# 256 rows of w2 by an indirect load to 64 chosen partitions, in a fused adaLN, cached attention and MLP decode step

## The chip, the cores and the metric

One core of a Trainium2 chip runs the whole program. The metric is device time in microseconds (us) of one execution, the median of several runs. The profiled execution is one more run, with its own time.

## What is computed

Eight tokens (one for each sequence, D = 512) go through attention over a window of a key and value cache and then through an MLP, each with an adaptive layer norm and a gate from a conditioning vector c.

```python
mod = (silu(c) @ w_mod).reshape(8, 6, 1, -1)            # sa, ca, ga, sb, cb, gb
h = layernorm(x) * (1 + ca) + sa
q = (h @ wq)                                             # 32 heads of 128
k, v = k_cache[:, :, Sk - W:], v_cache[:, :, Sk - W:]    # W = 2048 of 8192, 8 kv heads
o = softmax(q k^T * Dh ** -0.5) v
x = x + ga * (o @ wo)
h = layernorm(x) * (1 + cb) + sb
r = relu(h @ w1 + b1) ** 2                               # w1 [512, 1792]
x = x + gb * (r @ w2 + b2)                               # w2 [1792, 512]
```

All of it is float32. The caches' windows are 134 MB, the weights some 31 MB, and each byte is used once.

## The kernel before

Four slots of 4 MB in SBUF (`slots`) hold whatever is being used: two halves of w_mod, two of wq, then for each of the eight sequences two tiles of K and two of V, then wo (two tiles), w1 and w2. `load` issues the transfers of one such tile on SyncE's queue (SP), and `pump` issues the next tile of the list as soon as a slot comes free, so the order of all bulk transfers is the list `loads`. SP also waits for the completion of the transfer that used the same one of eight completion semaphores before.

The loop over b (line 431 on) overlaps three stages: turning K by 32x32 transposes on VectorE (`turn`), `scores` on TensorE with a block query matrix in `qb`, the softmax (`rows`, `maximum`, `exponent`, `divisor`, `spread`), and P times V of the sequence before (`turn_p`, `weighted`, `gather`).

The tail, from line 473 on, is: the product with wo; the residual and the second norm; h2T, the second norm's result with its columns turned onto partitions; `ph`, the hidden layer; relu, square, a 32x32 transpose (rT); and the product with w2.

The 1792 rows of w2 are held in two ways. The main part has FC rows on each of 128 partitions (FC = 13, 1664 rows, line 109), loaded in five pieces (line 110): f = 0 to 3, 4 to 7, 8 to 10, 11, 12. The other 128 rows are the extra part: four rows on each of 32 partitions, in `w2x`, the storage of the query matrices, which are dead after the last scores. A memset of Pool's (line 325) clears it first, and two transfers on SP (line 108, EXTRA) fill it. The hidden layer is split the same way: `ph` has the 13 x 32 columns of each quarter on 128 partitions, and `px` (line 529) has the extra 128 columns, with relus on ScalarE (line 545) and a transpose into rxT (line 555).

The product with w2 has three parts. (1) f = 0 to 3 and the four extra rows are eight products of 512 columns in four column groups of the array, which end in `wy_ps` (line 562); these are copied to `at_y` by VectorE (left half) and then by ScalarE (right half; lines 566 and 567) and summed over the four groups by products with `sel` (line 579). (2) f = 4 to 7 are products of 128 columns, one for each quarter of D, straight into `py` (line 572). (3) f = 8 to 12 are such quarters too, issued after the sums. `y` is py times the gate plus x1 (lines 585 and 586), and goes out by one transfer.

A product in float32 stands in the trace as two matrix instructions, so eight instructions are four products.

## Time and profile before

| | us |
|---|---|
| median of 3 runs (391.48 to 391.55) | 391.51 |
| the profiled execution | 391.81 |
| its span, first to last instruction | 390.0 |

| engine | busy us | share of the span |
|---|---|---|
| TensorE | 257.2 | 66% |
| VectorE | 215.7 | 55% |
| ScalarE | 42.8 | 11% |
| GpSimd (Pool) | 6.6 | 2% |
| SP's transfer queue, of 16 DMA engines | | 98.4% |

165.05 MB are moved, 423 GB/s over the span. A busy share is an average over stages; which wait ends last in a stage is read from the chain of waits and from the timeline. The granted clock is TensorE's; a share of 1.00 is 2.4 GHz, 0.50 is 1.2 GHz.

### The profile page before, as it was taken

Reading aid. Unit: us, or ns where it says so; the run is one execution under the profiler, and the core shown is the slowest. Engines: PE = TensorE matmul, PEld = TensorE weight load, DVE = VectorE, ACT = ScalarE, POOL = GpSimd, SP = SyncE. Lnnn points to the kernel's source line nnn. Section 1 sums busy time; section 2 is a strip of 40 time slices with the busy share of each in tenths; the row PEclk is TensorE's granted clock in tenths of the full one; section 3 lists DMA queues with packets and bytes.
Section 4 is the critical chain, followed back from the end, with each engine's and each line's share of the span. In section 5 each row is a group of like instructions: output and inputs, shape, how many; then the busy total and the mean of one; then the engine's idle time right before and its main releaser. Section 6 shows DMA issues by size and latency. Waiting matters only on the chain.

```text
span 390.0 us, 4820 instructions
## 1 busy us (share of the span) xinstructions
PE 257.2 (66%) x2126; PEld 111.1 (28%) x2126; DVE 215.7 (55%) x234; ACT 42.8 (11%) x91; POOL 6.6 (2%) x14
## 2 busy tenths in 40 slices
PE   0272808678975694859485938394749475985975
PEld 0120201151351343124322422233223313452332
DVE  3420199399394939293928391939292938330032
ACT  0310100030030003000300020003000300032010
POOL 4000000000000000000000000000000000100000
PEclk9998758969975986889778987797688779888889
DMA  8999999999999999999999999999999999999995
GB/s 325 432 434 428 430 430 434 434 444 439 435 437 428 427 432 434 430 428 430 429 430 428 434 430 432 437 439 430 439 434 434 426 437 425 434 435 413 424 421 207
DMA packets 7253, 165.05 MB, mean 423 GB/s; under 512 B 888, under 2 KB 1056, under 8 KB 1696
## 3 DMA queue, kind: packets, MB, share of 16 engines
q1 hardware_dynamic: 7096, 164.70, 98.4%
q8 instruction: 17, 0.28, 0.3%
q10 hardware_dynamic: 72, 0.04, 0.0%
q14 instruction: 4, 0.03, 0.0%
q0 software_dynamic: 64, 0.00, 0.0%
HBM read 164.67 MB, written 0.07 MB: 422 GB/s over the span
## 4 chain that ended last, share of the span: by engine, by line
DMA 53%; DVE 25%; PE 20%; ACT 1%; issue 1%; DVEq 0%; ACTq 0%; SPq 0%
DMA slot<-in_A_k_cache_dram 34%; DVE slot L307 22%; PE s_ps L317 16%; DMA slot<-in_B_w_dram 9%; DMA slot<-in_A_wq_dram 7%; DMA slot<-in_w_mod_dram 3%; PE t_ps L260 2%; PE t_ps L388 1%; PE o_ps L400 1%; PE m_ps L276 1%; DVE pT L389 0%; ACT prd L378 0%; DVE s L331 0%; DVE s L335 0%; DVE mx L340 0%
## 5 line engine op out<-in xcount | busy, mean ns | idle before, releaser
L307 DVE STREAM_TRANSPOSE slot<-slot 128x2048 f32<-128x2048 f32 x64 | 143.9, 2284 | 41.7 <-DMA slot<-in_A_k_cache_dram 41.7
L317 PE MATMUL s_ps<-slot,qb_all 128*32 128x512 f32 x512 | 121.7, 1099 | 68.4 <-DVE slot L307 67.5
L317 PEld LDWEIGHTS s_ps<-slot,qb_all 128*32 128x32 f32 x512 | 22.3, 136 | 147.7 <-issue 82.1
L400 PE MATMUL o_ps<-slot,pT 128*32 128x256 f32 x1024 | 59.7, 382 | 0.0
L400 PEld LDWEIGHTS o_ps<-slot,pT 128*32 128x32 f32 x1024 | 46.0, 112 | 27.7 <-issue 18.8
L388 PE MATMUL t_ps<-ident,prd 128*128 128x128 f32 x128 | 27.1, 373 | 16.5 <-ACT prd L378 9.5
L331 DVE STREAM_TRANSPOSE s<-s_ps 128x512 f32<-128x512 f32 x8 | 5.7, 717 | 54.2 <-PE s_ps L317 54.2
L388 PEld LDWEIGHTS t_ps<-ident,prd 128*128 128x128 f32 x128 | 20.2, 189 | 22.3 <-ACT prd L378 21.8
L378 ACT ACTIVATE prd<-pr,rz 128x512 f32<-128x512 f32 x32 | 20.5, 710 | 9.4 <-DVE rz L370 9.4
L354 ACT ACTIVATE pr<-s,nm 128x512 f32<-128x512 f32 x8 | 5.8, 722 | 141.2 <-DVE nm L348 141.2
L389 DVE TENSOR_TENSOR pT<-t_ps,m 128x512 f32<-128x512 f32 x32 | 20.4, 670 | 1.3 <-PE t_ps L388 1.2
L410 ACT COPY o_sb<-o_ps 128x256 f32<-128x256 f32 x16 | 5.8, 363 | 122.1 <-PE o_ps L400 122.1
L260 PE MATMUL t_ps<-slot,h1T 128*32 128x512 f32 x64 | 9.8, 764 | 8.9 <-DMA slot<-in_A_wq_dram 6.9
L475 PE MATMUL s_ps<-slot,oT 128*32 128x512 f32 x56 | 8.5, 773 | 4.5 <-DMA slot<-in_A_wo_dram 4.5
L173 PE MATMUL m_ps<-xsum,sel 128*128 128x1 f32 x2 | 0.6, 362 | 16.5 <-DVE xsum L196 16.5
L294 DVE TENSOR_TENSOR qb_all<-qrep,block 128x512 f32<-128x512 f32 x8 | 9.0, 1124 | 3.0 <-ACT qrep L286 3.0
L272 DVE STREAM_TRANSPOSE qT<-t_ps 128x512 f32<-128x512 f32 x2 | 1.4, 717 | 15.9 <-PE t_ps L260 15.7
L366 PE MATMUL m_ps<-z,same 128*128 128x1 f32 x16 | 3.3, 273 | 9.5 <-ACT pr L354 9.5
L238 PE MATMUL m_ps<-slot,cT 128*32 128x384 f32 x64 | 7.8, 658 | 0.0
L325 POOL MEMSET qb_all<- 64x2048 f32 x1 | 1.8, 1807 | 331.9 <-PE s_ps L317 331.9
L489 DVE COPY at_i<-s_ps 128x256 f32<-128x256 f32 x1 | 0.4, 425 | 12.2 <-PE s_ps L475 12.2
L260 PEld LDWEIGHTS t_ps<-slot,h1T 128*32 128x32 f32 x64 | 2.4, 133 | 16.1 <-DMA slot<-in_A_wq_dram 7.8
(113 smaller groups left out, 102.5 us busy)
## 6 DMA issues: line engine op xcount, KB each, us to landing
slot<-in_A_k_cache_dram SPq DMA_DIRECT2D x16, 4096.0 KB, 18.6
slot<-in_A_v_cache_dram SPq DMA_DIRECT2D x16, 4096.0 KB, 28.2
slot<-in_A_wq_dram SPq DMA_DIRECT2D x2, 4096.0 KB, 26.4
slot<-in_w_mod_dram SPq DMA_DIRECT2D x2, 3072.0 KB, 17.2
slot<-in_A_wo_dram SPq DMA_DIRECT2D x1, 4096.0 KB
slot<-in_A_wo_dram SPq DMA_DIRECT2D x1, 2048.0 KB
slot<-in_A_wo_dram SPq DMA_DIRECT2D x2, 1024.0 KB
slot<-in_B_w_dram SPq DMA_DIRECT2D x2, 1024.0 KB
```

Of the source, the lines that this page charges most:

```text
L238: nc.tensor.matmul(pm[i][32 * q : 32 * q + 32, : 3 * P].rearrange("p (m n) -> p m n", m=3), cT[:, kc, :], wm[:, 3 * i : 3 * i + 3, q, :], ...
L260: nc.tensor.matmul(pq[t][32 * x : 32 * x + 32, :], hT[:, kc, :], w[:, 2048 * t + 512 * x : 2048 * t + 512 * x + 512], start=(kc == 0), sto ...
L294: nc.vector.tensor_mul(qb[b % 2][:, :, :, :REP], qrep_b[:, :, None, :, b].to_broadcast([P, 32, 4, REP]), block[:, None, :, None].to_broadc ...
L307: nc.vector.transpose(k, k)
L317: nc.tensor.matmul(S_[b][32 * x : 32 * x + 32, :].rearrange("p (j i) -> p j i", i=8), q[:, n : n + 32], k[:, :, c, :, x], start=(t == 0 an ...
L354: nc.scalar.activation(pr.rearrange("p j (a i) -> p j a i", a=4), S2_.pop(b).rearrange("p (a j i) -> p j a i", a=4, i=8), AF.Exp, bias=NM_ ...
L378: nc.scalar.activation(d, pr[:, 4 * n : 4 * n + 4, :, None].to_broadcast([P, 4, 32, 4]), AF.Copy, scale=RZ_[b][0])
L388: nc.tensor.transpose(pp[:, P * i : P * i + P], d[:, i].rearrange("p i u -> p (i u)"), one)
L389: nc.vector.tensor_mul(PT_[b][:, n].rearrange("p q j (x r) -> p q (j x) r", r=REP), pp.rearrange("p (y q r) -> p q y r", y=16, r=REP), m16 ...
L400: nc.tensor.matmul(o[32 * (m % 4) : 32 * (m % 4) + 32].rearrange("p u d -> p (u d)"), PT_[b][:, n, 2 * q + t, 2 * u : 2 * u + 2, :].rearra ...
L410: nc.scalar.copy(O_[b][:, t], o)
L475: nc.tensor.matmul(wo_ps[32 * (i % 4) : 32 * (i % 4) + 32, :], oT[:, i, :], slot(("wo", i // 16), D)[:, i % 16, :], start=(i < 4), stop=(i ...
```

## The change

FC goes from 13 to 12, so the main part of w2 is 1536 rows in pieces f = 0 to 3, 4 to 7, 8 and 9, 10, 11, and the extra part is 256 rows: four on each of 64 partitions. These 64 are not a block: `EXTRA` names runs of partitions in the four groups of 32. The rows come by one indirect transfer of Pool's, behind a memset of all 128 partitions, right after the last scores; its list of row numbers (`places`) is made at the start by a memset and nine iotas of Pool's and two operations of VectorE's, and holds an out-of-range number for the 64 partitions that get nothing. SP's two transfers of extra rows go. The bias loads move from the program's start to ScalarE's queue in the second batch (b = 1).

In the tail, the product of b1_x comes before the hidden layer's loop; `px` has 256 columns on all 128 partitions; six relus take the place of two; the square and the transpose of rx come after both halves of r; f = 4 to 7 become products of 512 columns in `wy_ps`, eight in place of four of the main part; at_y is two tiles; f = 8 and 9 come before the sums, f = 10 and 11 after.

TensorE in the tail, before (s_ps is wy_ps, t_ps is ph and then py, m_ps is px; slot_90 holds w2):

```order
L520 MATMUL t_ps<-slot_91,h2T 32x416 x16
L527 MATMUL m_ps<-b_x,ident 64x128
L529 MATMUL m_ps<-slot_91,h2d 64x128 x4
L562 MATMUL s_ps<-slot_90,rT 32x512 x4
L562 MATMUL s_ps<-qb_all,rxT 32x512 x4
L569 MATMUL t_ps<-b_in,fours 128x128
L572 MATMUL t_ps<-slot_90,rT 32x128 x16
L579 MATMUL t_ps<-at_y,sel 32x128 x4
L572 MATMUL t_ps<-slot_90,rT 32x128 x20
```

and now (slot_87 holds w2):

```order
L550 MATMUL m_ps<-b_x,ident 128x256
L553 MATMUL t_ps<-slot_88,h2T 32x384 x16
L561 MATMUL m_ps<-slot_88,h2d 128x256 x4
L593 MATMUL s_ps<-slot_87,rT 32x512 x8
L593 MATMUL s_ps<-qb_all,rxT 32x512 x4
L600 MATMUL t_ps<-b_in,fours 128x128
L604 MATMUL t_ps<-slot_87,rT 32x128 x8
L611 MATMUL t_ps<-at_y_1825,sel 32x128 x2
L611 MATMUL t_ps<-at_y_1826,sel 32x128 x2
L604 MATMUL t_ps<-slot_87,rT 32x128 x8
```

Sixteen quarters of f = 4 to 7 have become four products of 512 columns, which stand ahead of the extra rows' four and of the sums. What these wait for now (DMAHW3 is the landing of w2's second piece, DMASW0 that of the indirect transfer):

```order
L593 MATMUL s_ps<-slot_87,rT 32x512 [waits DMAHW3_49]
L593 MATMUL s_ps<-slot_87,rT 32x512
L593 MATMUL s_ps<-slot_87,rT 32x512 [waits DVE_49]
L593 MATMUL s_ps<-slot_87,rT 32x512
L593 MATMUL s_ps<-qb_all,rxT 32x512 [waits DMASW0_49,DVE_49]
L593 MATMUL s_ps<-qb_all,rxT 32x512 x3
```

The extra rows' products, which before waited only for rxT and their own rows, are now behind the second piece of w2 too.

ScalarE at the end of the tail, before and now (rx is the extra part of r):

```order
L542 ACTIVATE relu<-t_ps 128x32x6
L542 ACTIVATE relu<-t_ps 128x32x7
L545 ACTIVATE rx<-m_ps 32x4x5x4
L545 ACTIVATE rx<-m_ps 32x4x3x4
L567 COPY at_y<-s_ps 128x256
```

```order
L574 ACTIVATE relu<-t_ps 128x32x6 [waits PE_49]
L574 ACTIVATE relu<-t_ps 128x32x6
L577 ACTIVATE rx<-m_ps 32x128 [waits PE_49,Pool_49]
L577 ACTIVATE rx<-m_ps 32x128
L577 ACTIVATE rx<-m_ps 32x24
L577 ACTIVATE rx<-m_ps 32x16 x3
L598 COPY at_y_1826<-s_ps 128x256 [waits DVE_49,Activation_49]
```

The relus are four more, and the copy of the right half of wy_ps waits, as before, for VectorE's copy of the left half, though the two now write two tiles.

SP's last transfers, before and now:

```order
L108 DMA qb_all<-in_B_w_dram 20x1x2048
L108 DMA qb_all<-in_B_w_dram 12x1x2048
L114 DMA slot_90<-in_B_w_dram 128x2048 x2
L114 DMA slot_90<-in_B_w_dram 128x1536
L114 DMA slot_90<-in_B_w_dram 128x512 x2
```

```order
L119 DMA slot_87<-in_B_w_dram 128x2048 x2
L119 DMA slot_87<-in_B_w_dram 128x1024
L119 DMA slot_87<-in_B_w_dram 128x512 x2
```

The extra rows are gone from SP's queue, and the third piece is a third shorter. The diff, cut to its core:

```diff
--- before.py
+++ after.py
@@ -41,7 +41,7 @@
     F = w1.shape[1]
     NJ = W // 32
     NQ = D // P
-    FC = F // P - 1
+    FC = F // P - 2
     FG = FC * 32
     FX = F - P * FC
     SCALE = float(DH) ** -0.5
@@ -61,15 +61,24 @@
     nc.vector.memset(xc_in, 0.0)
     for q in range(NQ):
         nc.scalar.dma_start(xc_in[32 * q : 32 * q + B], xc[32 * q : 32 * q + B])
-    b1_in = consts.tile([NQ, FG], F32, name="b1_in")
+    b1_in = consts.tile([NQ, FG + 32], F32, name="b1_in")[:, :FG]
     b1_x = consts.tile([1, FX], F32, name="b1_x")
     b2_in = consts.tile([NQ, P], F32, name="b2_in")
-    nc.scalar.dma_start(b1_in, b1[: P * FC].rearrange("(g n) -> g n", g=NQ))
-    nc.gpsimd.dma_start(b1_x, b1[P * FC :].rearrange("(g n) -> g n", g=1))
-    nc.gpsimd.dma_start(b2_in, b2.rearrange("(g n) -> g n", g=NQ))
-
-
-    EXTRA = ((0, 5, P * FC, 0), (32, 3, P * FC + 80, 80))
+
+
+    EXTRA = (
+        (0, 0, 12, 0),
+        (0, 16, 4, 16),
+        (0, 28, 4, 28),
+        (1, 0, 20, 32),
+        (1, 26, 6, 58),
+        (2, 0, 6, 52),
+        (2, 28, 4, 12),
+        (3, 0, 4, 20),
+        (3, 28, 4, 24),
+    )
+
+    SPAN = ((0, 0, 32, 0), (1, 0, 32, 32)) + EXTRA[5:]
     qb_all = consts.tile([P, 2, 32, 4, 8], F32, name="qb_all")
     w2x = qb_all.rearrange("p t n a z -> p (t n a z)")
 
@@ -102,12 +111,8 @@
             v = w1.rearrange(r_kc, p=P)
             pieces = [(lo, v[:, lo:hi]) for lo, hi in ((0, 2), (2, 3), (3, 4))]
         else:
-
-            for g, o, first, _ in EXTRA:
-                v = w2[first : first + 16 * o].rearrange("(i o c) n -> o i (c n)", i=4, o=o)
-                nc.sync.dma_start(w2x[g : g + 4 * o, :], v)
             v = w2[: P * FC].rearrange("(p c) n -> p c n", p=P)
-            cuts = ((0, 4), (4, 8), (8, 11), (11, 12), (12, 13))
+            cuts = ((0, 4), (4, 8), (8, 10), (10, 11), (11, 12))
             pieces = [(lo, v[:, lo:hi]) for lo, hi in cuts]
         for lo, v in pieces:
             a, n = v.shape[1:]
...
@@ -221,7 +226,22 @@
     qb = [qb_all[:, i] for i in range(2)]
     for t in qb:
         nc.gpsimd.memset(t, 0.0)
-    rx = consts.tile([64, 32, 4], F32, name="rx")
+
+    place_r = work.tile([P, 32], F32, name="mt", bufs=1)
+    nc.gpsimd.memset(place_r, float(F))
+    for g, l, n, first in EXTRA:
+        nc.gpsimd.iota(
+            place_r[32 * g : 32 * g + 1, l : l + n],
+            pattern=[[1, n]],
+            base=P * FC // 4 + first,
+            channel_multiplier=0,
+            allow_small_or_imprecise_dtypes=True,
+        )
+    place_c = work.tile([P, 32], F32, name="nm")
+    nc.vector.transpose(place_c, place_r)
+    places = consts.tile([P, 1], mybir.dt.uint32, name="places")
+    nc.vector.tensor_copy(places, place_c[:, 0:1])
+    rx = consts.tile([P, 32, 4], F32, name="rx")
     nc.gpsimd.memset(rx, 0.0)
     oT = consts.tile([P, 32, 32], F32, name="oT")
     nc.gpsimd.memset(oT, 0.0)
@@ -322,7 +342,15 @@
                     stop=(t == 1 and c == 3),
                 )
         if b == B - 1 and t == 1:
-            nc.gpsimd.memset(w2x[:64, :], 0.0)
+            nc.gpsimd.memset(w2x, 0.0)
+            nc.gpsimd.indirect_dma_start(
+                w2x,
+                None,
+                w2.rearrange("(r c) n -> r (c n)", c=4),
+                bass.IndirectOffsetOnAxis(ap=places[:, :1], axis=0),
+                bounds_check=F // 4 - 1,
+                oob_is_err=False,
+            )
         done(("K", b, t))
 
     def rows(b):
@@ -465,6 +493,10 @@
             exponent(b)
         else:
             nc.scalar.activation(warm, eps, AF.Sqrt)
+        if b == 1:
+            nc.scalar.dma_start(b1_in, b1[: P * FC].rearrange("(g n) -> g n", g=NQ))
+            nc.scalar.dma_start(b1_x, b1[P * FC :].rearrange("(g n) -> g n", g=1))
+            nc.scalar.dma_start(b2_in, b2.rearrange("(g n) -> g n", g=NQ))
         if b > 0:
             weighted(b - 1, 1)
     gather(B - 1)
@@ -507,14 +539,15 @@
     xm, rstd = norm(x1, x1sum)
     nc.vector.tensor_mul(xm, xm, mods[1][:, 1, :])
     h2T = scaled(xm, rstd, mods[1][:, 0, :], "h2T")
-    h2d = work.tile([P, NQ, 2, 32], F32, name="h2d", tag="prd", bufs=4)
-    nc.vector.tensor_copy(h2d, h2T[:, :, None, :].to_broadcast([P, NQ, 2, 32]))
+    h2d = work.tile([P, NQ, 4, 32], F32, name="h2d", tag="prd", bufs=4)
+    nc.vector.tensor_copy(h2d, h2T[:, :, None, :].to_broadcast([P, NQ, 4, 32]))
 
     w1t = slot(("w1",), F)
     w2t = slot(("w2",), D)
     ph = ps_t.tile([P, 512], F32, name="t_ps")
     px = bank()
     nc.tensor.matmul(ph[:, :FG], four, b1_in, start=True, stop=False)
+    nc.tensor.matmul(px[:, :FX], one[:1, :1].to_broadcast([1, P]), b1_x, start=True, stop=False)
     for kc in range(NQ):
         for g in range(NQ):
             nc.tensor.matmul(
@@ -524,10 +557,9 @@
                 start=False,
                 stop=(kc == NQ - 1),
             )
-    nc.tensor.matmul(px[:64, :FX], one[:1, :1].to_broadcast([1, 64]), b1_x, start=True, stop=False)
     for kc in range(NQ):
         nc.tensor.matmul(
-            px[:64, :FX],
+            px[:, :FX],
             h2d[:, kc].rearrange("p a b -> p (a b)"),
             w1t[:, kc, P * FC :],
             start=False,
@@ -535,51 +567,51 @@
         )
     r = work.tile([P, 32, FC], F32, name="relu", tag="a")
     rT = work.tile([P, FC, 32], F32, name="rT", bufs=1)
-    rxT = work.tile([64, 4, 32], F32, name="rxT", bufs=1)
+    rxT = work.tile([P, 4, 32], F32, name="rxT", bufs=1)
     h = ph[:, :FG].rearrange("p (l c) -> p l c", l=32)
     halves = ((0, 6), (6, FC))
     for lo, hi in halves:
         nc.scalar.activation(r[:, :, lo:hi], h[:, :, lo:hi], AF.Relu)
 
-    for g, o, _, at_ in EXTRA:
+    for g, l, k, first in SPAN:
         nc.scalar.activation(
-            rx[g : g + 32, : 4 * o, :].rearrange("p (o i) c -> p i o c", i=4),
-            px[g : g + 32, at_ : at_ + 16 * o].rearrange("p (i o c) -> p i o c", i=4, o=o),
+            rx[32 * g : 32 * g + 32, l : l + k, :],
+            px[32 * g : 32 * g + 32, 4 * first : 4 * (first + k)].rearrange("p (l c) -> p l c", c=4),
             AF.Relu,
         )
     for lo, hi in halves:
         nc.vector.tensor_mul(r[:, :, lo:hi], r[:, :, lo:hi], r[:, :, lo:hi])
         nc.vector.transpose(rT[:, lo:hi], r[:, :, lo:hi].rearrange("p l c -> p c l"))
-        if lo == 0:
-            nc.vector.tensor_mul(rx, rx, rx)
-            nc.vector.transpose(rxT, rx.rearrange("p l c -> p c l"))
+    nc.vector.tensor_mul(rx, rx, rx)
+    nc.vector.transpose(rxT, rx.rearrange("p l c -> p c l"))
 
 
     wy_ps = ps_s.tile([P, D], F32, name="s_ps")
-    chunks = [(rT[:, f, :], w2t[:, f, :]) for f in range(4)]
-    chunks += [(rxT[:, c, :], w2x[:64, D * c : D * c + D]) for c in range(4)]
+    chunks = [(rT[:, f, :], w2t[:, f, :]) for f in range(8)]
+    chunks += [(rxT[:, c, :], w2x[:, D * c : D * c + D]) for c in range(4)]
     for i, (left, right) in enumerate(chunks):
         nc.tensor.matmul(
-            wy_ps[32 * (i % 4) : 32 * (i % 4) + 32, :], left, right, start=(i < 4), stop=(i >= 4)
-        )
-    at_y = work.tile([P, D], F32, name="at_y", tag="a")
-    nc.vector.tensor_copy(at_y[:, : D // 2], wy_ps[:, : D // 2])
-    nc.scalar.copy(at_y[:, D // 2 :], wy_ps[:, D // 2 :])
+            wy_ps[32 * (i % 4) : 32 * (i % 4) + 32, :], left, right, start=(i < 4), stop=(i >= 8)
+        )
+    at_y = [work.tile([P, 2, P], F32, name=f"at_y{i}", tag="prd", bufs=4) for i in range(2)]
+    nc.vector.tensor_copy(at_y[0], wy_ps[:, : D // 2].rearrange("p (q n) -> p q n", q=2))
+    nc.scalar.copy(at_y[1], wy_ps[:, D // 2 :].rearrange("p (q n) -> p q n", q=2))
     py = ps_t.tile([P, 512], F32, name="t_ps")
     nc.tensor.matmul(py[:, :P], four, b2_in, start=True, stop=False)
+
     def quarters(f, last):
         for q in range(NQ):
             nc.tensor.matmul(
                 py[32 * q : 32 * q + 32, :P], rT[:, f, :], w2t[:, f, q * P : (q + 1) * P], start=False, stop=last
             )
 
-    for f in range(4, 8):
+    for f in range(8, 10):
         quarters(f, False)
     for q in range(NQ):
         nc.tensor.matmul(
-            py[32 * q : 32 * q + 32, :P], sel[:, :32], at_y[:, q * P : (q + 1) * P], start=False, stop=False
-        )
-    for f in range(8, FC):
+            py[32 * q : 32 * q + 32, :P], sel[:, :32], at_y[q // 2][:, q % 2, :], start=False, stop=False
+        )
+    for f in range(10, FC):
         quarters(f, f == FC - 1)
     y = work.tile([P, P], F32, name="y", bufs=1)
     nc.vector.tensor_mul(y, py[:, :P], mods[1][:, 2, :])
```

## Rows read from the trace of the kernel before

**Rows 1.** The chain of waits, its last pieces: start us, us, what.

```profile
376.05 10.34 DMA slot<-in_B_w_dram
...
386.43 0.47 PE t_ps L572 x8
...
386.93 0.30 DVE y L585
```

**Rows 2.** Stretches of the tail: us, busy time by engine, clock, DMA share, GB/s.

```profile
370.70:374.40 3.70, 1.64 (x8) 0.90 (x9) 2.28 (x10) 0.76 (x3) 0.00 (x0) 1.00 0.99 418
...
374.90:378.10 3.20, 3.20 (x24) 0.65 (x12) 0.00 (x0) 0.00 (x0) 0.00 (x0) 0.50 1.02 429
...
381.00:383.40 2.40, 2.40 (x22) 0.60 (x24) 1.84 (x5) 0.01 (x1) 0.00 (x0) 1.00 0.94 392
383.40:387.00 3.60, 2.77 (x81) 1.92 (x80) 0.19 (x2) 0.38 (x1) 0.00 (x0) 1.00 0.49 189
```

**Rows 3.** DMA issues: sizes in KB, and us from issue to landing.

```profile
slot<-in_A_k_cache_dram SPq DMA_DIRECT2D x16, 4096.0 KB, 18.6
...
slot<-in_B_w_dram SPq DMA_DIRECT2D x1, 768.0 KB
slot<-in_B_w_dram SPq DMA_DIRECT2D x2, 256.0 KB, 10.3
```

**Rows 4.** Timeline of PE in the tail: start us, us, instructions [idle before <-releaser].

```profile
378.57 0.53 PE L520 MATMUL t_ps<-slot,h2T 128*32 128x416 f32 x4
...
379.39 1.09 PE L529 MATMUL m_ps<-slot,h2d 128*64 128x128 f32 x8
380.96 1.07 PE L562 MATMUL s_ps<-slot,rT 128*32 128x512 f32 x8 [0.49 <-DMA slot<-in_B_w_dram]
381.96 1.06 PE L562 MATMUL s_ps<-qb_all,rxT 64*32 64x512 f32 x8
...
383.37 1.08 PE L572 MATMUL t_ps<-slot,rT 128*32 128x128 f32 x32
```

**Rows 5.** Timeline of ScalarE (ACT) and VectorE (DVE) in the tail.

```profile
380.57 0.44 ACT L545 ACTIVATE rx<-m_ps 32x80 f32<-32x80 f32 x2 [0.80 <-PE m_ps L529]
...
381.05 0.28 DVE L554 TENSOR_TENSOR rx<-rx 64x128 f32<-64x128 f32 x1 [0.58 <-ACT rx L545]
381.36 0.41 DVE L555 STREAM_TRANSPOSE rxT<-rx 64x128 f32<-64x128 f32 x1
...
383.09 0.42 DVE L566 COPY at_y<-s_ps 128x256 f32<-128x256 f32 x1 [0.45 <-PE s_ps L562]
...
383.61 0.38 ACT L567 COPY at_y<-s_ps 128x256 f32<-128x256 f32 x1 [2.59 <-DVE at_y L566]
```

**Rows 6.** Timeline near 45 us: eight matrix instructions with 128x128 weights and 256 columns.

```profile
45.67 1.99 PE L276 MATMUL m_ps<-qT,rep 128*128 128x256 f32 x8 [0.85 <-DVE qT L272]
```

**Rows 7.** Timeline of the product with wo and its sums, at full clock.

```profile
365.25 0.14 PEld L475 LDWEIGHTS s_ps<-slot,oT 128*32 128x32 f32 x4 [0.29 <-issue]
365.68 0.13 PEld L475 LDWEIGHTS s_ps<-slot,oT 128*32 128x32 f32 x4 [0.29 <-issue]
...
368.97 0.37 ACT L490 COPY at_i<-s_ps 128x256 f32<-128x256 f32 x1 [14.24 <-DVE at_i L489]
...
369.39 0.14 PEld L493 LDWEIGHTS m_ps<-at_i,sel 128*32 128x32 f32 x4 [0.26 <-ACT at_i L490]
...
369.58 1.10 PE L498 MATMUL m_ps<-slot,oT 128*32 128x128 f32 x32
370.73 0.29 DVE L505 TENSOR_TENSOR x<-m_ps,mod 128x128 f32<-128x128 f32 x1 [1.79 <-PE m_ps L498]
```

**Rows 8.** Timelines: start of the program, second batch, and just after the last scores.

```profile
3.07 0.32 ACTq L67 DMA_DIRECT2D b_in<-in_B_b_dram  x1
...
111.50 1.95 ACT L378 ACTIVATE prd<-pr,rz 128x512 f32<-128x512 f32 x3 [1.23 <-DVE rz L370]
...
337.85 1.81 POOL L325 MEMSET qb_all<- 64x2048 f32 x1 [331.91 <-PE s_ps L317]
```

More of the change, by code (lines that the diff above doesn't have):

```diff
@@ L199, in tile_adaln_cached_attention_mlp @@
     nc.scalar.activation(warm, eps, AF.Exp)
-    rep = consts.tile([P, 4, 4, 32], F32, name="rep")
+    rep = work.tile([P, 4, 4, 32], F32, name="rep", tag="prd", bufs=4)
     nc.vector.tensor_copy(
```

## The prediction

> **What bounds the kernel now.** I read the chain of waits first. Its last pieces are a transfer of w2 that lands at 386.39 (376.05 + 10.34), eight matrix instructions of the last quarter at 386.43, and y at 386.93 [rows 1]. So the end is the last landing plus 0.54 us up to y, and what follows y is not touched. The stretches of the tail say how that transfer ends: from 374.9 to 378.1 the 16 DMA engines are all busy (share 1.02 at 429 GB/s), from 381.0 to 383.4 the share is 0.94, and from 383.4 to 387.0 only 0.49 [rows 2]. The engines run dry one after another: 0.49 of 3.6 us is 1.76 us of work for all sixteen, so with the same bytes shared evenly the last would land near 383.4 + 1.76 = 385.16 and not at 386.39. That is the most that a better sharing can give, 1.2 us. The timeline then shows what TensorE, ScalarE and VectorE have to do between the landings [rows 4, 5].
>
> **The change, part by part.**
>
> *The transfers.* Bytes are the same. The main part of w2 loses one row in thirteen, 256 KB, all in the third piece (768 KB before [rows 3], 512 now); these and the 256 KB of the old extra part become the indirect load's 512 KB. For an engine that gets none of the 64 rows that is 16 KB less behind the second piece; an engine moves 429 / 16 = 26.8 GB/s [rows 2], so it ends 0.61 us sooner, and a row of 8 KB costs an engine 0.31 us. If the engines that end last now get none or few of the rows, the last landing goes from 386.39 to 385.78. I take this; the bounds are 385.16 (even sharing) and 388.2 (eight rows, 2.45 us, on an engine that is among the last now, less 0.61).
>
> The second piece ends where it did, since it and all before it in SP's queue are unchanged on those engines. It has landed by 383.37, when its first quarter product runs [rows 4], and not much sooner: 768 + 256 + 256 KB lie behind it [rows 3], which is 1.31 MB or 3.05 us at 430 GB/s before 386.39, so 383.34.
>
> *Pool.* The memset is as wide per partition as before (1.81 us from 337.85 [rows 8]), so the indirect load is issued near 340, and its rows are wanted after 384: whatever Pool needs to work out 64 rows is hidden by 40 us. The iotas, and VectorE's two small operations, stand in the first 20 us, where bulk loads run anyway.
>
> *The biases.* Three issues on ScalarE at about 0.32 us each [rows 8] come to 1.0 us in the second batch. ScalarE sat idle for 1.23 us there [rows 8], but its copy of the output tile is now behind them, and TensorE's gather behind that, so up to 1 us of one batch may move. A K tile lands 18.6 us after its issue [rows 3], while moving its own 4.19 MB takes 9.8 us at 429 GB/s: some 9 us are queued ahead, and that cover hides it. Were it gone, the cost would be that 1 us.
>
> *The extra part of the hidden layer.* w1's last piece is no later, so px's products start near 379.0, the end of the last products of L520 (378.57 + 0.53 = 379.10 [rows 4], less 0.06 for 384 in place of 416 columns). Eight instructions with 128x128 weights and 256 columns took 1.99 us [rows 6], where px takes 1.09 [rows 4]: it ends at 381.0. The relu follows 0.09 us after the end (380.48 to 380.57 [rows 4, 5]); two took 0.44, six take 1.32, up to 382.4. Square, transpose and their two gaps take 0.72 (381.05 to 381.77 [rows 5], and 0.04 before): rxT is ready at 383.2, against 381.77 before. That is 1.4 us later, but the extra rows' products are now behind f = 4 to 7, which can't start before 383.37 and stream for 0.86 us. So I cost this at nothing; the slack is 384.2 - 383.2 = 1.0 us.
>
> *The products of 512 columns.* This is what now ends late. f = 4 to 7 start at 383.37, and the extra rows' four follow. In the trace eight instructions at 381.96 let VectorE's copy go at 383.09, 1.13 us [rows 4, 5]; eight more, streamed, add 2 x 0.43 us (the pace of four, 365.25 to 365.68 [rows 7]): 383.37 + 1.13 + 0.86 = 385.36. The copy of the left half and the wait behind it take 0.52 (383.09 to 383.61) and ScalarE's copy of the right half 0.38 [rows 5]: 386.26. Two tiles don't make these run side by side, since the order shows the second still waiting for VectorE.
>
> *The sums and the last quarters.* The same step after wo: the copy ends at 369.34, the sum's second half starts at 369.39, and VectorE's next operation at 370.73, 1.34 us, with 32 instructions of quarters in 1.10 us behind the sum [rows 7]. Now 16 follow (f = 10 and 11), 0.55 less: 0.79. So y starts at 386.26 + 0.05 + 0.79 = 387.10, against 386.93: **0.2 us later**. By the transfer alone it would be 385.78 + 0.54 = 386.32, so the landing that ended the kernel is now hidden by 0.8 us and the chain from w2's second piece ends it.
>
> **The sum.** 391.51 + 0.2 = 391.7. The sum is made on the profiled execution, whose 391.81 would become 392.0; the median is 0.30 below it. Terms I am unsure of by some tenths are the landing of the second piece and the pace of the copies. A measurement of this kernel can tell 0.2%, 0.78 us, from no change: the forecast lies within that.
>
> **The rivals.**
>
> *The landing still ends it.* If the chain behind the second piece is 0.8 us shorter than I make it, the end is the last landing: 391.5 - 0.6 = 390.9, still within 0.2%. To be faster by more, the sharing must come out nearly even and the chain short as well: 385.16 + 0.54 gives 390.3. Against it: 0.42, 0.38 and the pace of the products are rows, not guesses. Chance 12% for the first, 6% for over 0.2%.
>
> *The clock falls in the gap.* TensorE now has nothing to do from the end of f = 0 to 3 (about 382.0) to 383.37, where before the extra rows' products ran from 381.96 to 383.02 [rows 4]. From 370.7 to 374.4 it was busy for 1.64 of 3.70 us at clock 1.00, and from 374.9 to 378.1 the granted clock was 0.50, the lower of its two levels, 1.2 GHz [rows 2]. Should that come again at 383.4, the four streams of 0.43 us take 0.86 (1.72 more) and the last step about 0.5 more: y at 389.3, so 393.9, slower. It decides as soon as the clock is 0.50 in the stretch from 383.4 to 385.4. For it: less work ahead of the critical products than before. Against it: the gap is 1.3 us, after some 4 us that are nearly full. Chance 12%.
>
> *The rows fall on the wrong engines.* Nothing in the rows tells which DMA engine serves which partition. Spread evenly, four rows on each engine, each bulk landing behind 340 us would come up to 1.2 us later on the engines that end last, w2's second piece at 384.6, and y at 388.3: 392.9. With eight rows on an engine among the last, 2.45 later, y at 389.5: 394.1. It decides from two rows (0.6 us) on a late engine on. Chance 12%.
> The Trainium skill (DMA: Bandwidth & Descriptors, The descriptor swizzle) gives a rule for the engine of a partition in a transfer to 128 partitions; by it seven engines (0, 1, 2, 4, 7, 8, 15) get eight of the 64 rows, one four, two two and six none, and the sum stays as it is if those six are the late ones. The same page (Latency and other measured facts) says that engines 7 and 15 are usually the slower ones in traces, by its best guess because of transfers that Pool issues; both get the full eight here, so by that rule this rival holds, at 394.1. No row of this trace parts the engines, so it agrees with neither.
>
> *It does nothing.* The stream is full until 383.4 either way, and if both ends shift by under 0.3 us it reads as no change. That is my forecast's neighbour and shares its 58%.
>
> **How the numbers follow.** Within 0.2%: the forecast and its neighbour 58%, the landing rival 12%, together 0.70. Slower: the clock 12%, the engines 12%, 0.24. Faster 0.06. The likeliest case's own range is 391.3 to 392.2. For 8 in 10 the range goes down to 390.9 (the landing ends it) and up to 393.5, past even spreading (392.9); left out are the far end of the two slower rivals and the faster case.
>
> **What would show it.** In the profile after: w2's last landing near 385.8 and no longer in the chain's last pieces; the chain ending in the second piece of w2, L593, the copies at L597 and L598, L611 and L604; VectorE's copy near 385.4; rxT near 383.2; clock 1.00 from 383.4 on; the DMA share falling in one step rather than over 3.6 us. I am wrong if the second piece lands later than 383.7 (the engines), if the clock is at 0.50 there, or if the last instructions still wait for a transfer.

## The result, and the profile after

The changed kernel takes **392.16 us** (median of 22 runs, 392.01 to 392.48), the kernel before 391.63 (22 runs, 391.42 to 391.91): 0.53 us more, a ratio of 1.0015 with a 95% interval of 1.0008 to 1.0021. That is within the 0.2% of the forecast. The profiled executions stand 0.30 us apart (392.11 after, 391.81 before).

The chain of waits after (start us, us, what) ends otherwise than [rows 1]:

```profile
360.28 23.06 DMA slot<-in_B_w_dram
...
383.39 1.92 PE s_ps L593 x16
...
386.73 0.46 PE t_ps L604 x14
...
387.21 0.30 DVE y L617
```

The transfer in it is w2's second piece, landed at 383.34; what follows is 3.87 us of products, copies and sums up to y. The last landing is no longer there. The last piece of w2 is issued at 369.98 and lands 15.9 us later, near 385.9, where before it landed at 386.39 [rows 1] (start us, us, what; then the size and the us from issue to landing):

```profile
369.98 0.33 SPq L119 DMA_DIRECT2D slot<-in_B_w_dram  x1
slot<-in_B_w_dram SPq DMA_DIRECT2D x1, 256.0 KB, 15.9
```

Stretches of the tail (us, busy time by engine, clock, DMA share, GB/s), first after, then before:

```profile
378.10:381.00 2.90, 2.90 (x24) 1.59 (x16) 1.17 (x4) 0.56 (x2) 0.00 (x0) 1.00 1.01 421
...
384.00:385.00 1.00, 1.00 (x16) 0.13 (x4) 0.00 (x0) 0.00 (x0) 0.00 (x0) 1.00 0.84 324
385.00:386.00 1.00, 1.00 (x18) 0.64 (x18) 0.42 (x1) 0.11 (x1) 0.00 (x0) 1.00 0.11 41
386.00:387.00 1.00, 1.00 (x36) 0.81 (x28) 0.00 (x0) 0.27 (x1) 0.00 (x0) 1.00 0.00 0
```

```profile
385.00:386.00 1.00, 0.85 (x32) 0.77 (x32) 0.00 (x0) 0.00 (x0) 0.00 (x0) 1.00 0.44 170
```

The sharing did what the change set out to do: the share falls from 0.84 to 0.11 to nothing, where before it was still 0.44 in the us from 385. The steps of the tail, from the timeline (beside [rows 4, 5]):

```profile
379.25 1.99 PE L561 MATMUL m_ps<-slot,h2d 128*128 128x256 f32 x8
381.34 1.07 ACT L577 ACTIVATE rx<-m_ps 32x128 f32<-32x128 f32 x6 [1.39 <-PE m_ps L561]
382.77 0.40 DVE L586 STREAM_TRANSPOSE rxT<-rx 128x128 f32<-128x128 f32 x1
383.39 1.06 PE L593 MATMUL s_ps<-slot,rT 128*32 128x512 f32 x8 [1.15 <-DMA slot<-in_B_w_dram]
384.27 1.04 PE L593 MATMUL s_ps<-qb_all,rxT 128*32 128x512 f32 x8
385.38 0.42 DVE L597 COPY at_y<-s_ps 128x256 f32<-128x256 f32 x1 [2.21 <-PE s_ps L593]
385.89 0.37 ACT L598 COPY at_y<-s_ps 128x256 f32<-128x256 f32 x1 [3.48 <-DVE at_y L597]
387.21 0.29 DVE L617 TENSOR_TENSOR y<-t_ps,mod 128x128 f32<-128x128 f32 x1 [1.41 <-PE t_ps L604]
```

The parts costed at nothing, from the timeline and the list of DMA issues (the last number is us to landing):

```profile
109.33 0.72 ACT L382 ACTIVATE pr<-s,nm 128x512 f32<-128x512 f32 x1 [20.01 <-DVE nm L376]
109.33 0.26 ACTq L497 DMA_DIRECT2D b_in<-in_B_b_dram  x1
111.63 1.95 ACT L406 ACTIVATE prd<-pr,rz 128x512 f32<-128x512 f32 x3 [1.02 <-DVE rz L398]
339.98 1.16 POOL L346 DMA_INDIRECT qb_all<-in_B_w_dram,places  x1 [0.29 <-POOL qb_all L345]
qb_all<-in_B_w_dram,places POOLq DMA_INDIRECT x1, 17.3
369.96 0.81 PEld L530 LDWEIGHTS m_ps<-slot,oT 128*32 128x32 f32 x32 [0.28 <-DMA slot<-in_A_wo_dram]
```

and the exponent of the same batch before:

```profile
109.19 0.72 ACT L354 ACTIVATE pr<-s,nm 128x512 f32<-128x512 f32 x1 [20.01 <-DVE nm L348]
```

ScalarE's next operation in the second batch starts at 111.63 against 111.50 [rows 8]; but the exponent ahead of it had already started 0.14 later (109.33 against 109.19), so these 0.13 us are not the bias issues'. The indirect load has its rows in place near 357, 27 us before they are used. One thing moved that had been costed at nothing: TensorE waits until 369.96 for the last piece of wo, where before it ran these products at 369.58 [rows 7], and everything up to ph's loop is 0.38 later (374.77 against 374.39). e2 below, which loads no chosen rows, runs these products at 369.48. No term of the prediction had this delay; the slack that it gives the hidden layer's way takes it up.

### The profile page after: what moved, and what is told of

Read it like the earlier page. It is cut to its first block, busy times and chain, and to the rows that moved or that the text cites. A ratio compares the mean times of both kernels' runs of the same rounds, so it can differ in the third digit from the quotient of the medians.

```text
span 390.3 us, 4769 instructions
## 1 busy us (share of the span) xinstructions
PE 256.3 (66%) x2094; PEld 116.2 (30%) x2094; DVE 216.0 (55%) x236; ACT 43.5 (11%) x95; POOL 7.7 (2%) x23
## 4 chain that ended last, share of the span: by engine, by line
DMA 55%; DVE 24%; PE 19%; issue 1%; ACT 0%; SPq 0%; DVEq 0%; ACTq 0%
DMA slot<-in_A_k_cache_dram 34%; DVE slot L327 22%; PE s_ps L337 16%; DMA slot<-in_A_wq_dram 9%; DMA slot<-in_B_w_dram 6%; DMA slot<-in_A_wo_dram 6%; PE t_ps L280 1%; PE m_ps L296 1%; PE t_ps L416 1%; PE s_ps L593 0%; DVE pT L417 0%; SPq L119 0%; PE t_ps L604 0%; ACT qrep L306 0%; ACT prd L406 0%
## 5 line engine op out<-in xcount | busy, mean ns | idle before, releaser
L337 PEld LDWEIGHTS s_ps<-slot,qb_all 128*32 128x32 f32 x512 | 23.8, 135 | 145.6 <-issue 80.0
L428 PEld LDWEIGHTS o_ps<-slot,pT 128*32 128x32 f32 x1024 | 49.3, 112 | 24.6 <-issue 17.6
L345 POOL MEMSET qb_all<- 128x2048 f32 x1 | 1.8, 1806 | 332.3 <-PE s_ps L337 332.3
```

Of the source, the lines that this page charges most:

```text
L337: nc.tensor.matmul(S_[b][32 * x : 32 * x + 32, :].rearrange("p (j i) -> p j i", i=8), q[:, n : n + 32], k[:, :, c, :, x], start=(t == 0 an ...
L428: nc.tensor.matmul(o[32 * (m % 4) : 32 * (m % 4) + 32].rearrange("p u d -> p (u d)"), PT_[b][:, n, 2 * q + t, 2 * u : 2 * u + 2, :].rearra ...
```

## The experiments

All were timed against the kernel before on the same chip, which there took 391.58 to 391.62 in the median. The changed kernel did not run beside them; where one of them is set against its 392.16, that rests on the kernel before taking the same (391.63) beside it.

**Undo the products of 512 columns (e1_quarters).**

```diff
-    chunks = [(rT[:, f, :], w2t[:, f, :]) for f in range(8)]
+    chunks = [(rT[:, f, :], w2t[:, f, :]) for f in range(4)]
...
-    for f in range(8, 10):
+    for f in range(4, 10):
```

> The changed kernel with one part undone: f = 4 to 7 are sixteen products of 128 columns again, and only f = 0 to 3 and the extra rows go through the copies and sums. Theory A (the chain from the second piece of w2 through four streams of 512 columns and two copies in a row ends the kernel): the copies now start near 384.4 and end near 385.3, before the last landing at 385.85, so the end is that landing plus 0.54: y at 386.4, 0.8 us sooner than in the changed kernel, 391.3 against its 392.16, and 0.3 to 0.5 below the kernel before. Theory B (the indirect load and the moved biases cost the time somewhere ahead of the tail): no better than the kernel before, 391.6 or more.

Measured 393.04 (ten runs, 391.76 to 394.17), ratio 1.0028 (1.0016 to 1.004). Neither theory. The chain of the profiled execution (393.31) holds no transfer in its last 16 us:

```profile
375.33 5.28 PE t_ps L553 x32
380.60 1.95 PE m_ps L561 x8
...
384.06 0.41 DVE rxT L586
...
384.52 1.07 PE s_ps L593 x8
...
386.00 1.45 PE t_ps L604 x48
```

```profile
378.10:381.00 2.90, 2.90 (x18) 0.83 (x11) 0.00 (x0) 0.33 (x2) 0.00 (x0) 0.57 1.01 424
```

The second fence is a stretch: the granted clock was 0.57 there, 1.00 in the changed kernel. TensorE's programs are the same up to that point; at the lower level ph's and px's products end 1.3 us later, rxT comes at 384.47 instead of 383.17, and 24 quarter products queue behind it. Even its best run, 391.76, is no better than before, which suggests that something beside the clock holds it up too: e6 finds it.

**The products alone (e2_products_alone): the kernel before, with f = 4 to 7 in 512 columns.**

```diff
-    chunks = [(rT[:, f, :], w2t[:, f, :]) for f in range(4)]
+    chunks = [(rT[:, f, :], w2t[:, f, :]) for f in range(8)]
...
-    for f in range(4, 8):
+    for f in range(8, 11):
...
-    for f in range(8, FC):
+    for f in range(11, FC):
```

> The kernel before with one part of the change alone: f = 4 to 7 by products of 512 columns, f = 8 to 10 ahead of the sums, f = 11 and 12 behind. Transfers, extra rows and biases as before. Theory A: the second piece lands near 383.3 as ever, the copy by VectorE starts near 385.36 and y near 387.15 against 386.93, so 0.2 to 0.3 us over the kernel before, 391.85 to 391.95. Theory B: as the kernel before, within 0.1 us.

Measured 391.96 (391.82 to 392.8), ratio 1.001 (1.0001 to 1.0019): 0.34 more than before, at the upper end of what A has. Without any change of transfers, the products move the end to w2's second piece; the chain of its profiled execution runs from that landing at 383.06 through L562, and not from the last. That execution is one of the slower (392.52), and the trace says why: the clock was 0.68 from 378.1 to 381.0, the second half of rT came late, and two of the four products behind the landing had to wait for it:

```profile
383.10 1.60 PE L562 MATMUL s_ps<-slot,rT 128*32 128x512 f32 x8 [0.56 <-DMA slot<-in_B_w_dram]
383.65 0.14 PEld L562 LDWEIGHTS s_ps<-slot,rT 128*32 128x32 f32 x4 [0.41 <-DVE rT L552]
```

1.60 us stand there in place of 1.06 in the changed kernel. Less these 0.54, y would start at 387.09 and not 387.63, near A's 387.15.

**Other partitions (e3_block_64_127): all the rows on 64 to 127.**

```diff
...
-    SPAN = ((0, 0, 32, 0), (1, 0, 32, 32)) + EXTRA[5:]
+    EXTRA = ((2, 0, 32, 0), (3, 0, 32, 32))
+    SPAN = EXTRA
```

> The changed kernel with the 256 rows on partitions 64 to 127 as a block (two relus in place of six; all else as it is). Theory A (a partition decides which DMA engine writes it, and the 64 chosen partitions belong to the engines that run dry first): engines among the last now get eight rows, 2.45 us each, so the pieces of w1 and w2 land up to 2.4 us later, and y is near 389.6: 394.5. Rival C (the engine is not decided by the partition, or the engines do not differ): the landings stay, and four relus fewer change nothing on the path: 392.1 to 392.2.

Measured 394.09 (393.99 to 394.39), ratio 1.0064 (1.0051 to 1.0077). A holds, at 1.9 us where it had up to 2.4: the choice of partitions alone does it. The delay comes in well ahead of w2, as the last products with wo show (e3's row, then that of the changed kernel, whose 52 all end at 368.59):

```profile
369.36 1.06 PE L497 MATMUL s_ps<-slot,oT 128*32 128x512 f32 x8 [0.25 <-DMA slot<-in_A_wo_dram]
```

```profile
361.18 7.41 PE L507 MATMUL s_ps<-slot,oT 128*32 128x512 f32 x52
```

e3 waits for wo until 369.36 and ends these products at 370.42, 1.83 later. w2's second piece is as late: TensorE loads the weights for its products at 385.31, 1.93 later than in the changed kernel (383.38), and y stands at 389.14, 1.93 later too.

```profile
385.31 0.16 PEld L583 LDWEIGHTS s_ps<-slot,rT 128*32 128x32 f32 x8 [0.79 <-DMA slot<-in_B_w_dram]
```

The chain of this execution names px as the last to come before these products (it ended at 384.44, at a clock of 0.50 from 378.1 to 381.0); the two ways are within some tenths of each other there, and which of them set the end is not shown. The transfers also trail: the share is 0.55, 0.37 and 0.40 in the three us from 384 on, the last of them a stretch in which the changed kernel moves nothing:

```profile
386.00:387.00 1.00, 1.00 (x12) 0.17 (x8) 0.00 (x0) 0.00 (x0) 0.00 (x0) 1.00 0.40 154
```

The Trainium skill (DMA: Bandwidth & Descriptors, The descriptor swizzle) says which engine serves which partitions in a transfer to all of them; by it, partitions 64 to 127 belong to engines 8 to 15, eight rows each, if it holds for the indirect load's rows too. A tail at 0.4 agrees with about half of the engines being loaded; no row here names an engine.

**One copy (e4_one_copy): one VectorE copy of 512 columns.**

```diff
-    nc.vector.tensor_copy(at_y[0], wy_ps[:, : D // 2].rearrange("p (q n) -> p q n", q=2))
-    nc.scalar.copy(at_y[1], wy_ps[:, D // 2 :].rearrange("p (q n) -> p q n", q=2))
+    nc.vector.tensor_copy(at_y, wy_ps.rearrange("p (q n) -> p q n", q=4))
```

> The changed kernel with one copy of 512 columns by VectorE in place of two copies of 256 that run one after the other (0.42, a wait of 0.1, 0.37). A 128x512 operation of VectorE took 0.67 to 0.72. Theory A: the sums start some 0.2 us sooner, y near 387.0: 391.9 to 392.0. Theory B: no change, 392.1 to 392.2.

Measured 392.02 (391.92 to 392.34), 0.14 below the changed kernel's median; from the landing to y 3.71 us in place of 3.87. That is what A has: the two copies do run one after the other, and that term lies on the path, though the two medians' spreads overlap.

**Spare products in TensorE's gaps (e5_fill_after: the changed kernel; e6_fill_quarters: e1).** `busy(t, n)` issues n products `matmul(t[:, :P], one, one, start=True, stop=True)`; ph's tile, which the real products overwrite, is taken earlier.

```diff
+    ph = ps_t.tile([P, 512], F32, name="t_ps")
+    busy(ph, 2)
     pw = bank()
...
-    xm, rstd = norm(x1, x1sum)
+    xm, rstd = norm(x1, x1sum, ph, (3, 3))
```

> The changed kernel with eight spare 128x128 products on TensorE in the idle gaps of 368.6 to 373.0 us (two behind wo's 512-column products, three ahead of each of the two norm sums; their result is overwritten and used by nothing). Theory A (the changed kernel ends with the second piece of w2, landing at 383.34 us, plus its products, copies and sums): the granted clock may stay at 1.00 from 374 us on, rxT comes earlier than 383.17 us, but the time stays 392.1 to 392.2. Rival D (the stretch at half clock from 374.6 to 378.0 us is on the path of the changed kernel): 391.0 to 391.6. If the clock falls all the same, nothing follows for D.

> The kernel of e1_quarters with the same eight spare products. Theory A (e1_quarters missed because its clock stayed at 0.50 until 380 us and more, so that w1's last products, the six relus and rxT came late, with 24 quarter products queued behind them): the clock stays up, rxT comes by 383.2 us, the last landing near 385.85 us ends the work and y starts near 386.5; 391.1 to 391.4, with the spread of ten runs below 0.5 us. Rival E (quarter products of f = 4 to 7 behind the copies cost the time by themselves, whatever the clock does): 392.5 to 393.2, as in e1_quarters.

e5 took 392.14 (392.02 to 392.4), as the changed kernel; its clock fell to 0.50 from 375 to 378 all the same, so it says nothing on D. e6 took **391.81** (391.66 to 392.0): 1.2 us below e1 and with a spread of 0.34 in place of 2.4, and the clock of its profiled execution was 1.00 from 370.7 us on. So far A. But it is not 391.1, and the chain says why:

```profile
378.62 0.04 issue
378.66 0.85 PE t_ps L562 x8
379.51 1.94 PE m_ps L570 x8
...
382.96 0.41 DVE rxT L595
...
383.41 1.07 PE s_ps L602 x8
384.48 0.41 PE t_ps L609 x2
384.89 1.45 PE t_ps L613 x48
...
386.56 0.48 PE t_ps L613 x16
...
387.06 0.30 DVE y L626
```

What lands at 378.62 is the last piece of w1. From there px, six relus, rxT and TensorE's own queue lead to y at 387.06 with no transfer of w2 between: a third way to the end, 0.15 us shorter than that of the changed kernel.

**Quarters ahead of rxT (e7_quarters_first).**

```diff
+    for f in range(4):
+        nc.tensor.matmul(
+            wy_ps[32 * f : 32 * f + 32, :], rT[:, f, :], w2t[:, f, :], start=True, stop=False
+        )
+    nc.tensor.matmul(py[:, :P], four, b2_in, start=True, stop=False)
+    for f in range(4, 8):
+        quarters(f, False)
...
```

> The changed kernel with f = 4 to 7 as 16 quarter products again, but issued between the products of f = 0 to 3 and the four products of the chosen rows, so that they do not queue behind rxT. Theory A: the second piece still bounds; 16 quarters take about 0.85 us in place of four products of 1.06 us, so 391.9 to 392.1 where rxT comes by 384 us, up to 392.5 where the half clock lasts to 380 us. Rival E (the quarter form itself costs): 392.5 to 393.2.

Measured 392.35 (392.09 to 393.35), eleven runs: six from 392.09 to 392.35, as A allows at most, and five from 392.81 to 393.35, as E has it. The profiled execution is the one at 393.35, with the clock at 0.50 until past 380 us and the chain through ph and px, so it doesn't show what ends the other six. Inconclusive, except that this order is no gain.

**Biases at the start (e8_biases_at_start).**

```diff
+    nc.scalar.dma_start(b1_in, b1[: P * FC].rearrange("(g n) -> g n", g=NQ))
+    nc.gpsimd.dma_start(b1_x, b1[P * FC :].rearrange("(g n) -> g n", g=1))
+    nc.gpsimd.dma_start(b2_in, b2.rearrange("(g n) -> g n", g=NQ))
...
-        if b == 1:
-            nc.scalar.dma_start(b1_in, b1[: P * FC].rearrange("(g n) -> g n", g=NQ))
...
```

> The changed kernel with the three bias loads at the program's start, on the queues where the kernel before has them (one of ScalarE's, two of Pool's). Theory A (that move was costed at nothing): 392.1 to 392.2, as the changed kernel. Rival F (Pool's two more issues at the start, ahead of its zeroing and the indices, delay the first batch): 392.4 or more; (the loads in the second batch cost their 1.0 us of ScalarE): 391.2 to 391.7.

Measured 392.32 (392.2 to 392.75), ratio 1.002 (1.0011 to 1.0029): between what A and F have, with an interval that overlaps that of the changed kernel. The profiled execution, the lowest of the eleven, has the same chain, y at 387.18. The loads in the second batch cost nothing, and may save 0.1 or 0.2.

**px between ph's products (e9_px_between: on e6; e10_px_between_no_fill: on e1; e11_px_between_products: on e5).** The product of each k for px moves into ph's loop over k, behind the four of ph:

```diff
                 stop=(kc == NQ - 1),
             )
-    for kc in range(NQ):
         nc.tensor.matmul(
             px[:, :FX],
```

> The kernel of e6_fill_quarters with the product of each k for the 256 extra columns issued right behind the four products of ph for the same k, so that three of the four run before w1's last piece has landed (378.62 us in e6). Theory G (in e6 the way from w1's last piece over px, six relus, rxT and the four products of the chosen rows to the quarter products ended the work, 383.37 to 387.06 us, and not the last landing near 385.85): where the clock stays up px ends 1.5 us earlier, rxT comes by 382.4 to 382.6, the last landing ends the work and y starts by 386.5; 391.1 to 391.4, faster than the kernel before. Rival H (something behind the copies, the 24 quarter products and the sums, sets the end whatever comes before): 391.7 to 391.9 as e6.

> e9_px_between without the eight spare products. Theory G with the clock as in the changed kernel (0.50 for 3.4 us or twice that from about 374 us on): TensorE is then busy without a gap from 374.8 us, and moving px earlier gives rxT only about 0.5 us or nothing; 391.6 to 392.2 in most runs, some at 392.5 to 393.2 where the half clock lasts longer. Rival (the spare products do nothing, the order of px alone does it): as e9_px_between, 391.1 to 391.4 in nearly all runs.

> e9_px_between with f = 4 to 7 as four products of 512 columns, as the changed kernel has them. Theory A (these products, which wait for w2's second piece at 383.34 us and stand ahead of the copies, end the changed kernel): rxT comes earlier but the time stays 392.1 to 392.2. Rival I (the late rxT ends the changed kernel): 391.1 to 391.5, as e9.

e9 took 391.62 (twelve runs), in two groups: seven from 391.27 to 391.62, five from 392.71 to 392.86. The first group is 0.2 to 0.5 us below e6: four of the seven are at 391.42 or less, as G asks, and none is at 391.7 or more, as H has it. The profiled execution is of the second (392.82), and its clock fell while TensorE was running products almost without a gap:

```profile
374.40:375.00 0.60, 0.50 (x6) 0.16 (x8) 0.57 (x2) 0.00 (x0) 0.00 (x0) 1.00 1.05 442
375.00:376.00 1.00, 1.00 (x8) 0.00 (x0) 0.23 (x1) 0.00 (x0) 0.00 (x0) 0.51 0.98 409
```

At that level the px products only stand ahead of ph's last ones, and rxT comes at 384.26. e10, without spare products, took 394.13 (392.66 to 394.27), a miss: I had allowed for 393.2. Its profiled clock was 0.50 from before 374.4 to beyond 380 us and ph's last products ended near 382.9, so both halves of rT came late as well, and rxT at 385.66. e11 took 392.48 (392.07 to 393.62), above A's range by 0.3 and far from I's. Its profiled execution, the slowest of nine, had the clock at 1.00 from 370.7 us to the landing and rxT ready at 382.62, and the chain still ran from w2's second piece: the late rxT is not what ends this form, and neither is a lower clock ahead of it, which was e5's rival D. But the stretch behind that landing looked like this:

```profile
381.00:383.40 2.40, 1.07 (x8) 0.16 (x8) 1.56 (x5) 0.64 (x5) 0.00 (x0) 1.00 0.99 411
383.40:385.00 1.60, 1.55 (x12) 0.45 (x16) 0.00 (x0) 0.00 (x0) 0.00 (x0) 0.60 0.87 338
385.00:386.00 1.00, 1.00 (x12) 0.14 (x4) 0.00 (x0) 0.00 (x0) 0.00 (x0) 0.50 0.08 29
```

```profile
383.45 3.43 PE s_ps L601 x16
```

The clock was 1.00 until the landing and fell just behind it, after TensorE had been busy for 1.07 of 2.40 us; the sixteen instructions took 3.43 us where the changed kernel's take 1.92. What the other eight runs lost is not shown.

**The bias product earlier (e12_bias_product_early), on e6.**

```diff
     for i, (left, right) in enumerate(chunks):
+        if i == 4:
+            nc.tensor.matmul(py[:, :P], four, b2_in, start=True, stop=False)
```

> The kernel of e6_fill_quarters with the bias product of py (0.41 us on TensorE's way in e6, at 384.48 us) issued between the products of f = 0 to 3 and those of the chosen rows, where TensorE waited from 382.3 to 383.4 us. Theory G (in e6 the end is TensorE's own queue behind rxT: four products, the bias product, 24 quarter products, sums, 8 quarter products): y starts 0.4 us earlier, near 386.65, with the last landing's own bound near 386.5 just below; 391.3 to 391.5 in the runs whose clock stays up. Rival H (the copies or the last landing end e6, and the bias product lies beside them): 391.7 to 391.9.

Measured **391.35** (eleven runs, 391.21 to 391.45): 0.46 below e6, 0.81 below the changed kernel, and 0.25 below the 391.6 of the kernel before, though the ratio's interval, 0.9984 to 1.0003, still holds 1. The chain confirms G:

```profile
383.23 1.06 PE s_ps L605 x8
384.30 1.31 PE t_ps L614 x48
...
385.83 0.55 PE t_ps L614 x16
...
386.40 0.30 DVE y L627
```

The 0.41 us of the bias product are gone from between the first two rows. y comes at 386.40, 0.66 earlier than in e6, of which 0.18 were there already when the chosen rows' products began (383.23 against 383.41). More than this a change of order can't give here, for the last landing is now as near to y as in the kernel before:

```profile
369.96 0.33 SPq L119 DMA_DIRECT2D slot<-in_B_w_dram  x1
slot<-in_B_w_dram SPq DMA_DIRECT2D x1, 256.0 KB, 15.9
```

The last piece of w2 lands at 369.96 + 15.9, near 385.86, and y follows 0.54 behind, as it did before (386.39 to 386.93 [rows 1]).

## Why the prediction was right

**The transfers.** Right: I had the last landing at 385.78, 0.61 us earlier, and it came near 385.9, 0.5 earlier; the share is down to 0.11 between 385 and 386 and 0.00 behind it. The second piece lands at 383.34, the number forecast; that it fits to the hundredth is luck, since it landed at 383.31 to 383.48 in the profiled executions of e4, e5, e8 and e11. What I left out is that wo's last piece comes later with the chosen rows and puts ph's loop back by 0.38 us.

**Pool and the biases.** Right. The indirect load took Pool 1.16 us and landed 27 us ahead of its use. The three issues took 0.26 us each rather than 0.32 and lay under ScalarE's own exponent, and nothing of them came through to the next operation; e8 shows no gain from undoing the move.

**The extra part of the hidden layer.** The result was right, two terms off, and by luck they cancel. px ended 0.24 later than I had it, because ph's loop began later and ended at 379.32 and not at 379.04. The six relus took 1.07 us instead of 1.32: I had priced all six like the two of before, but four of them have 16 or 24 columns. So rxT came at 383.17 against 383.2. Hidden in the changed kernel, as forecast. But the slack of 1.0 us was against the products of f = 4 to 7 only. Behind them this part is a way of its own: take the products away and it ends the kernel, at the better clock (e6, y at 387.06) and all the more at the lower one (e1, 388.17). I called this 1.4 us of delay free; with the products undone, it is what keeps the earlier landing from being worth anything.

**Products, copies and sums.** This was the step that decided, and its terms held: VectorE's copy at 385.38 (385.36 forecast), ScalarE's end at 386.26 (386.26), y at 387.21 (387.10). The 0.1 missing is in the last term: from the copy's end to y 0.95 us, not 0.84. e2 puts a price on the products by themselves, 0.34 of the 0.53 us in the medians. The other 0.2 is not assigned; in e2's trace the second piece lands 0.28 ahead of the changed kernel's (383.06 and 383.34), which would be enough, but these are one execution each. e4's shorter copy gets 0.14 of the whole back.

**The sum.** 0.2 us forecast, 0.30 measured between the profiled executions, 0.53 between the medians. So 392.16 is 0.46 above the 391.7 forecast, still inside the likeliest case's own range (up to 392.2), but at its edge. Of the 0.46, 0.12 are the base, 391.51 from three runs where 22 give 391.63; 0.1 is the last term above; and 0.23 come from the profiled executions, of which the one before lies 0.18 above its median and the one after 0.05 below. I took the first of these distances to be the same on both sides (0.30, from the three runs). Why it was not is not known; one execution of each has a timeline.

**The rivals.** That the landing still ends it: no, it is out of the chain. That the rows fall on the wrong engines: not with this choice, but e3 shows the mechanism and a price of 1.9 us. I had it delaying w2's pieces; it delays wo's already, and by about as much. The Trainium skill (DMA: Bandwidth & Descriptors, Latency and other measured facts) takes engines 7 and 15 to be usually slower, by which 394.1 would have come; 392.16 and the last landing near 385.9, where the prediction's bound for this case was 388.2, speak against that here, as far as the rows went to the engines by that page's rule. That the clock falls in the gap: not in the changed kernel's profile (1.00 from 378.1 on), but e11's shows exactly this, in 393.62 us, with 1.51 us on the products where I had put 1.72, and y at 388.76 for 389.3. What I had not listed is the lower clock staying longer ahead of 381 us, which made rxT 1.3 us later in e1. The changed kernel has 1.1 us of slack there (383.17 to 384.27), so it should lose little by it; e1, e9 and e10 have none. That the scatter of their runs comes from the clock is shown for the profiled executions alone.

**Where the 0.6 us of the earlier landing went.** Three ways to y lay within a us of each other: w2's last landing (near 385.9, so y at 386.4; of the profiled executions only e12's reached it), w2's second piece with its products (387.21), and w1's last piece over px and rxT (387.06 in e6). The change shortened the first, and its own parts lengthened the other two. e12, which takes both of these out of the way with the help of the eight spare products, has y at 386.40, 0.53 ahead of the kernel before: the whole of the earlier landing, of which its median shows 0.25.

## What to carry to other kernels

Before a transfer at the end is shortened, work out every way to the end as a sum of its own, and ask which of them the change itself makes longer: here three ended within a us, and it lengthened two. A step that is hidden behind another one of the same change is free only as long as that one stays; cost it against the next bound too. Then look for work that waits in an engine's queue behind something late and needs nothing late itself: moving one bias product by one place took 0.46 us off e6, and made it the only version whose median is below that of the kernel before, though by less than the interval can tell from nothing.

## What was not expected of the hardware

- Which partitions a load of 512 KB goes to moves the whole kernel by 1.9 us (e3 against the changed kernel), and the delay shows first in transfers that were issued for another tensor (wo, 1.8 us). Even the partitions chosen here put wo's last piece back by some 0.4.
- The granted clock differed between executions in which TensorE had run the same program: 0.57 against 1.00 from 378.1 to 381.0 in e1 and the changed kernel. With eight spare products in the gaps it stayed at 1.00 from 370.7 us on in the profiled executions of e6 and e12, until 383.4 in that of e11, and fell to 0.50 by 375 in those of e5 and e9.
- A relu on 32 partitions costs by its number more than by its columns: of the six now, two of 128 columns took 0.27 us each and three of 16 took 0.17 each.
